# Filter products of the first batch on VectorE alone, its conversions and last inverse pair moved, second batch's units one step earlier

## Chip, cores and metric

The kernel runs on one core of a Trainium2 chip. The metric is the device time of one execution in microseconds, the median of several runs. Engines are named as in the profile: PE is TensorE (matmuls), DVE is VectorE, ACT is ScalarE, POOL is GpSimd, SP is the SyncE queue that issues most DMAs.

## The reference

Two stages in a row. The first is a global filter: a real FFT over the sequence, a product with a complex filter, and the inverse FFT. The second is an MLP with a hard-swish between two matrix products.

```python
# x (8, 3008, 256), filt_r and filt_i (1505, 256)
X = np.fft.rfft(x, axis=1)
Y = X * (filt_r + 1j * filt_i)[None]
y = np.fft.irfft(Y, n=3008, axis=1).reshape(24064, 256)
# w_in (256, 2048), w_out (2048, 256)
h = y @ w_in
g = h * np.clip(h + 3.0, 0.0, 6.0) / 6.0
out = g @ w_out
```

All inputs and the output are float32.

## The kernel before

**The transform.** 3008 is split as 47 x 64. For each of the 8 batches the first transform runs over the 47 (`a_unit`, eight chunks c for each batch; in batch 0 `a0_unit` and `turn`), its result goes to DRAM (`z_store`, tile `t1`, two buffers) and comes back in another order (`t2_load`, six chunks). Twelve `b_unit`s do the second transform, two frequencies each; `f_unit` multiplies by the filter (products of real and imaginary halves into s1 and s2), `y_unit` adds the products, `bi_unit` does the first inverse transform of a pair of units, and `g_store` writes it to DRAM. `t4_load` and `n_unit` bring it back and produce the tokens in `xn`.

**The MLP.** The tokens are handled in 47 blocks of 512 (k), each in 8 steps (p) over 256 hidden units. So there are 376 steps, counted i = 8k + p. Block 0 uses plain products (`plain_up`, `plain_down`, `plain_out`), the others a seven-product scheme (`up_1` to `up_5`, `g_sums`, `down`, `out_1` to `out_5`). In a step PE does the up product of this step and the down product of the step before. `relu` on ACT and `hswish` on DVE lie between. `store` writes a finished block to the output with up to 15 DMAs on SP; block 0's is issued in step 8.

**The weights.** Each of the 16 halves of the weights is loaded as raw bits (`w_load`) and converted by seven or eight DVE instructions (`w_ops`, L245 to L270); `w_abs` takes one of them over to ACT. POOL then forms sums of weight parts (`w_sums`, L277).

**What sets the order.** The order is written out by hand: each engine executes its instructions in the order in which the program issues them, and the DMAs of SP, ACT and POOL stand in those engines' own order. Before step 0 comes the opening: batch 0's transforms, and direct products (`direct`, `n_first`) for the first tokens. For batch 0 the filter products are split: ACT copies PSUM to SBUF (L400), POOL makes s1 (L401), DVE makes s2 (L402, L403). One conversion (w1) is issued an instruction at a time between the units of this stage, through the generator `between`; three more follow the opening. Later work is put into steps by `at(step, fn, ...)`. Functions in `EARLY` come after the up products of their step, all others at its end. For batch 1 (`places`, n == 1) the `a_unit`s lie in steps 3 to 10, the first three b units in 13, 14 and 15, and each `z_store` is issued on SP at the end of its `a_unit`'s step; `t2_load` comes a step after the last `a_unit`.

**The functions around the change.** `a0_unit` (L330), `turn` (L342), `b_unit` (L384), `f_unit`, `near` and `y_unit` (L423 to L427), `bi_unit` (L438, copies L441), `g0_first` (L448), `g_store` (L455), `t4_load` (L481), `direct` (L512), `n_first` (L519, L521), `z_store` (L373), `t2_load` (L377), `x_load` (L300), and the main program from L744 on. In steps, L537 is the up product, L563 a sum on DVE that occurs once per step from step 8 on, L587 the hard-swish, L613 the down product (L624 and L635 in block 0), L690 the output store.

Of the kernel before, what the change touches and what calls it, by code (L numbers as in the profile page):

```python
# [10 lines left out]
FP32 = mybir.dt.float32  # L11
I32 = mybir.dt.int32
AXT = mybir.ActivationFunctionType
# [10 lines left out]
NA = 47  # L24
# [90 lines left out]
def kernel(  # L115
# [117 lines left out]


    def w_conv(i):
        for _ in w_ops(i):
            pass

    def w_ops(i):
        words = st.pop(("bits", i)).rearrange("p (n two) -> p n two", two=2)  # L240
        lo, hi = words[:, :, 0], words[:, :, 1]
        big, rest = (yp.tile([P, 2, D], FP32, name="y").bitcast(I32).rearrange("p a n -> p (a n)") for j in range(2))
        v = nc.vector
        high = st.pop(("high", i), None)
        v.tensor_scalar(out=big, in0=hi, scalar1=3, scalar2=0x3FFFFFFF,  # L245
                        op0=ALU.logical_shift_left, op1=ALU.bitwise_and)
        yield
        v.scalar_tensor_tensor(out=big, in0=hi, scalar=top_c, in1=big,  # L248
                               op0=ALU.bitwise_and, op1=ALU.bitwise_or)
        yield  # L250
        v.tensor_scalar(out=rest, in0=big, scalar1=23, scalar2=23,
                        op0=ALU.logical_shift_right, op1=ALU.logical_shift_left)
        yield
        v.tensor_scalar(out=lo, in0=lo, scalar1=9, scalar2=0x3F800000,
                        op0=ALU.logical_shift_right, op1=ALU.bitwise_or)
        yield
        if high is None:
            v.tensor_scalar(out=hi, in0=hi, scalar1=1, scalar2=1,
                            op0=ALU.logical_shift_left, op1=ALU.logical_shift_right)
            high = hi.bitcast(FP32)  # L260
            yield
        rest, big = rest.bitcast(FP32), big.bitcast(FP32)
        v.scalar_tensor_tensor(out=rest, in0=lo.bitcast(FP32), scalar=1.0, in1=rest,  # L263
                               op0=ALU.subtract, op1=ALU.mult)
        yield
        v.scalar_tensor_tensor(out=rest, in0=rest, scalar=2.0 ** -20, in1=big, op0=ALU.mult, op1=ALU.add)
        yield

        two = lambda t: t.rearrange("p (a d) -> p a d", a=2)
        v.scalar_tensor_tensor(out=w_part(i)[1], in0=two(high), scalar=1.125 * 2.0 ** -15, in1=two(rest),  # L270
                               op0=ALU.is_ge, op1=ALU.mult)
        yield

    def w_sums(i, late):
        w = (w_in, w_out)[i % 2][i // 2]
# [50 lines left out]
    def a0_unit(j):  # L326
        for dh in range(2):
            ps = bank(0)
            for u in range(4):
                nc.tensor.matmul(ps[:, ts(u, P)], x0[0:64 + NA, j + u, ts(dh, P)], st["start"][0:64 + NA, ts(1, P)],  # L330
                                 start=True, stop=True)
            copy(dh and j not in (8, 12), zt(dh).rearrange("p (n j) -> p j n", j=HC)[:, j:j + 4, :],
                 ps.rearrange("p (j n) -> p j n", j=4)[:, :, 0:4 * KH])
# [54 lines left out]
    def f_unit(b, i):  # L388
        c, r = divmod(2 * i, TC)
        ps = st.pop(("ps", b, i))  # L390
        f = st["ft", b, c][:, r:r + 2, :]

        pool_, n1, n2 = (hp, "h0", "h1") if b == 0 and i & 2 else (sp, "s1", "s2")
        s1, s2 = (pool_.tile([P, 512], FP32, name=n).rearrange("p (u d) -> p u d", u=2) for n in (n1, n2))

        re, im = slice(0, HALF), slice(HALF, P)
        if b == 0:

            xf = rp.tile([P, 512], FP32, name="r", tag="r").rearrange("p (u d) -> p u d", u=2)
            nc.scalar.activation(out=xf, in_=ps, func=AXT.Copy)  # L400
            nc.gpsimd.tensor_tensor(out=s1, in0=xf, in1=f, op=ALU.mult)  # L401
            nc.vector.tensor_tensor(out=s2[re], in0=ps[re], in1=f[im], op=ALU.mult)  # L402
            nc.vector.tensor_tensor(out=s2[im], in0=ps[im], in1=f[re], op=ALU.mult)  # L403
        elif near(b, i):
            for s, part, to, x_ in (s1, re, re, re), (s1, re, im, im), (s2, im, re, im), (s2, im, im, re):
                nc.vector.tensor_tensor(out=s[to], in0=ps[x_], in1=f[part], op=ALU.mult)  # L406
        else:
            nc.vector.tensor_tensor(out=s1, in0=ps, in1=f, op=ALU.mult)
            nc.vector.tensor_tensor(out=s2[re], in0=ps[re], in1=f[im], op=ALU.mult)
            nc.vector.tensor_tensor(out=s2[im], in0=ps[im], in1=f[re], op=ALU.mult)  # L410
        st["y", b, i] = s1, s2


    def near(b, i):
        return b == 1

    def y_unit(b, i):
        s1, s2 = st["y", b, i]
        y = yp.tile([P, 2, D], FP32, name="y") if b else rp.tile([P, 512], FP32, name="r", tag="r").rearrange(
            "p (u d) -> p u d", u=2)  # L420
        re, im = slice(0, HALF), slice(HALF, P)
        if near(b, i):
            nc.gpsimd.tensor_tensor(out=y[re], in0=s1[re], in1=s2[re], op=ALU.subtract)  # L423
            nc.gpsimd.tensor_tensor(out=y[im], in0=s1[im], in1=s2[im], op=ALU.add)
        else:
            nc.vector.tensor_tensor(out=y[re], in0=s1[re], in1=s1[im], op=ALU.subtract)
            nc.vector.tensor_tensor(out=y[im], in0=s2[re], in1=s2[im], op=ALU.add)  # L427
        st["y", b, i] = y


    def bi_unit(b, i):
        ys = [st.pop(("y", b, i + v)) for v in range(2)]
        ps = [psF.tile([P, 2, D], FP32, name="psf", tag="f") for ri in range(2)]
        for v, ri in ((0, 0), (1, 0), (0, 1), (1, 1)):

            products = isinstance(ys[v], tuple)
            w, y = (wi[:, 1 + ri, :], ys[v][ri]) if products else (wi[ts(ri, 64), 0, :], ys[v][ts(ri, 64)])
            nc.tensor.matmul(ps[ri][ts(v, 64)], w, y, start=True, stop=True)  # L438
        t = t3p.tile([P, 2, 2, D], FP32, name="t3")
        for ri in range(2):  # L440
            nc.scalar.activation(out=t[:, ri, :, :], in_=ps[ri], func=AXT.Copy)  # L441
        st["t3", b, i] = t

    def g0_first(i):
        t = st["t3", 0, i]
        for v in range(2):
            for h in range(2):
                nc.scalar.dma_start(g0_d[ds(h * HC, NJ + 1), :, ds(2 * (i + v), 2), :].rearrange("c ri u d -> c ri (u d)"),  # L448
                                    t[ds(v * 64 + h * HC, NJ + 1)].rearrange("p ri u d -> p ri (u d)"))

    def g_store(b, i):
# [251 lines left out]
    with tc.manual_schedule():  # L703
# [16 lines left out]
        def load_bits(most):  # L720
            nonlocal loaded
            while loaded < most and w_before(loaded) < done:
                w_load(loaded, nc.sync)
                loaded += 1
# [38 lines left out]
        nc.sync.dma_start(wai[:, 0:8, :], wai_d[:, 0:8, :])  # L763
        load_bits(4)
        turn(0)
        between = w_ops(1)
        next(between)
        for c in range(NT):
            for i in (2 * c, 2 * c + 1):
                b_unit(0, i)  # L770
                f_unit(0, i)
                next(between, 0)
                if c == NT - 1:
                    y_unit(0, i)
            if c + 1 < NT:
                turn(c + 1)
            if c:
                bi_unit(0, 2 * c - 2)
                (g0_first if c == NT - 1 else lambda i: g_store(0, i))(2 * c - 2)
            if c == 4:  # L780
                t4_load(0, 0, KH - 3 * TC, 1)
        t4_load(0, KH - 3 * TC, KH - TC, 1)
        done = 2
        for i in 2, 3:
            w_abs(i)
        direct(NU - 2)
        direct(NU - 1)
        load_bits(8)
        nc.sync.dma_start(wa, wa_d)
        n_first()  # L790
        bi_unit(0, NU - 2)
        for i in NU - 4, NU - 2:
            g_store(0, i)
        w_abs(4)
        convert(3)
        for i in range(1, done):
            w_sums(i, False)

        def wai_load():
            nc.sync.dma_start(wai[:, 8:HC, :], wai_d[:, 8:HC, :])  # L800

        at(0, x_load, 1, 0)

        for i, s in enumerate((0, 1, 1, 2, 3, 3, 4, 4, 5, 5, 6)):
            at(s, convert_one)
# [26 lines left out]
        def places(n):  # L832
            k = first[n]
            u = [NU - 1 - i for i in range(NU)]
            b_at = [(k - 2 - j // 3) * NP + 6 - 2 * (j % 3) for j in u]

            bi_at = [b_at[i] + (5 if i % 6 == 1 else 3) for i in range(NU)]
            a_at = [(k - 7 + c // 4) * NP + (0, 2, 5, 7)[c % 4] for c in range(NB)]
            if n == 1:
                a_at = list(range(3, NB + 3))  # L840
                b_at = [13, 14, 15, 18, 19, 20, 21, 22, 26, 27, 28, 29]
                bi_at = [i + 3 for i in b_at]
            return a_at, b_at, bi_at

# [122 lines left out]
```

## Time and profile before

| what | value |
|---|---|
| median of 3 runs | 2744.99 us (2744.37 to 2745.23) |
| the profiled execution | 2745.02 us |
| its span | 2743.2 us |
| mean granted clock of PE | 0.995 |
| PE busy | 2701.6 us |
| DVE busy | 1954.4 us |
| ACT busy | 1335.9 us |
| POOL busy | 437.1 us |

The span is the stretch from the first to the last instruction of the profiled execution, and all times below are counted from its start. A busy time is the sum over an engine's instructions; an engine that is busy is not always at its peak. A line of the timeline gives start, duration, engine, source line, operation, tiles (written tile before the arrow), and in brackets how long the engine had been idle and what released it. A line of the windows gives, for one stretch, the busy time of PE, its weight load, DVE, ACT and POOL, then PE's granted clock, the DMA engines' share and the rate in GB/s.

### The profile page before, as it was taken

What the parts mean: (1) busy time and instruction counts of PE and PEld (TensorE: products, weight loads), DVE (VectorE), ACT (ScalarE), POOL (GpSimd) and SP (SyncE); (2) the same over time, 40 slices, a digit from 0 to 9 for tenths busy, and PEclk for the clock granted to TensorE, in tenths of its full rate; (3) what the DMA queues carried; (4) which work ended last, traced back from release to release, by engine and by line L of the source; (5) the groups of instructions that cost most, each with busy time, mean ns of one, the idle gap of its engine ahead of it and who ended that gap; (6) DMA issues with size and microseconds to landing.
All of it is one profiled execution on the core that took longest, in us unless ns stands there. A gap on an engine that the chain in (4) does not pass through costs nothing.

```text
span 2743.2 us, 47103 instructions
## 1 busy us (share of the span) xinstructions
PE 2701.6 (98%) x18100; PEld 2403.2 (88%) x18100; DVE 1954.4 (71%) x3384; ACT 1335.9 (49%) x2673; POOL 437.1 (16%) x634
## 2 busy tenths in 40 slices
PE   8989999999999999999999999999999999999998
PEld 5578888998899988999889998899988999999997
DVE  7958756777567875678756777577775777766665
ACT  4344455445554455444554455544545444544443
POOL 4513321101211012100121001210012100100000
PEclk9999999999999999999999999999999999999999
DMA  8633233221332113321233212332123321100000
GB/s 216 199 94 94 57 89 89 72 58 46 85 90 77 50 48 92 90 69 50 56 87 99 66 42 63 87 98 69 39 57 91 92 72 39 42 24 24 19 9 16
DMA packets 119645, 195.88 MB, mean 71 GB/s; under 512 B 21561, under 2 KB 82681, under 8 KB 119105
## 3 DMA queue, kind: packets, MB, share of 16 engines
q1 hardware_dynamic: 101627, 148.14, 19.0%
q0 software_dynamic: 17152, 44.23, 7.0%
q8 instruction: 143, 2.34, 0.4%
q14 instruction: 81, 0.66, 0.1%
q10 hardware_dynamic: 642, 0.51, 0.1%
HBM read 120.86 MB, written 71.93 MB: 70 GB/s over the span
## 4 chain that ended last, share of the span: by engine, by line
PE 93%; DVE 4%; DMA 1%; issue 1%; ACT 0%; POOL 0%; SPq 0%; POOLq 0%; DVEq 0%; ACTq 0%
PE po L613 41%; PE al L537 23%; PE be L537 17%; PE psn L491 4%; PE psf L384 2%; PE psf L361 2%; PE psf L438 2%; DVE s L406 1%; DVE g L587 1%; DMA w_all<-in_x_dram 0%; DVE y L263 0%; DMA out_dram<-o 0%; DVE g L594 0%; PE psn L512 0%; DVE y L248 0%
## 5 line engine op out<-in xcount | busy, mean ns | idle before, releaser
L613 PEld LDWEIGHTS po<-w_all,g 128*128 128x128 f32 x10304 | 1369.2, 192 | 145.5 <-issue 38.9
L613 PE MATMUL po<-w_all,g 128*128 128x128 f32 x10304 | 1400.8, 276 | 2.6 <-DVE g L587 2.4
L587 DVE SCALAR_TENSOR_TENSOR g<-r,h 128x512 f32<-128x512 f32 x736 | 511.9, 696 | 278.1 <-ACT r L582 266.5
L582 ACT ACTIVATE r<-h,half_c 128x512 f32<-128x512 f32 x736 | 531.1, 722 | 326.7 <-DVE h L563 314.7
L537 PE MATMUL al<-xt,w_all 128*128 128x256 f32 x2208 | 661.4, 381 | 9.0 <-ACT s L558 6.8
L563 DVE TENSOR_TENSOR h<-be,s 128x512 f32<-128x512 f32 x368 | 254.1, 690 | 258.6 <-PE be L537 240.4
L537 PE MATMUL be<-xn,w_all 128*128 128x256 f32 x1472 | 437.8, 379 | 0.0
L537 PEld LDWEIGHTS al<-xt,w_all 128*128 128x128 f32 x2208 | 335.7, 192 | 11.5 <-issue 9.1
L537 PEld LDWEIGHTS be<-xn,w_all 128*128 128x128 f32 x1472 | 279.7, 190 | 37.9
L577 ACT ACTIVATE h<-al 128x256 f32<-128x256 f32 x368 | 141.4, 384 | 350.8 <-PE al L537 350.8
L568 DVE TENSOR_TENSOR h<-al,s 128x256 f32<-128x256 f32 x368 | 156.2, 425 | 165.9 <-PE al L537 164.5
L595 DVE TENSOR_TENSOR g<-g 128x512 f32<-128x512 f32 x368 | 257.2, 699 | 12.6
L558 ACT ACTIVATE s<-al 128x256 f32<-128x256 f32 x368 | 141.4, 384 | 197.7 <-PE al L537 197.7
L549 ACT ACTIVATE s<-be 128x256 f32<-128x256 f32 x368 | 141.4, 384 | 176.3 <-PE be L537 176.3
L537 PE MATMUL al<-xn,w_all 128*128 128x256 f32 x736 | 219.9, 381 | 0.5 <-ACT h L577 0.5
L537 PE MATMUL be<-xt,w_all 128*128 128x256 f32 x736 | 218.9, 379 | 0.0
L373 POOL DMA_DIRECT2D z_tmp<-t x192 | 110.7, 580 | 414.6 <-ACT t L364 412.2
L548 ACT ACTIVATE s<-al 128x256 f32<-128x256 f32 x368 | 141.4, 384 | 71.0 <-PE al L537 71.0
L594 DVE TENSOR_TENSOR g<-g 128x256 f32<-128x256 f32 x368 | 162.5, 442 | 12.6
L597 DVE TENSOR_TENSOR g<-g 128x256 f32<-128x256 f32 x368 | 161.0, 438 | 12.5
L669 POOL TENSOR_TENSOR o<-p,o 128x256 f32<-128x256 f32 x45 | 32.7, 727 | 796.2 <-ACT t L441 421.7
L537 PEld LDWEIGHTS be<-xt,w_all 128*128 128x128 f32 x736 | 139.8, 190 | 18.9
(139 smaller groups left out, 1923.1 us busy)
## 6 DMA issues: line engine op xcount, KB each, us to landing
g_tmp<-t POOLq DMA_DIRECT2D x96, 256.0 KB, 3.8
t<-g_tmp SPq DMA_DIRECT2D x188, 120.0 KB
t<-z_tmp SPq DMA_DIRECT2D x42, 512.0 KB
z_tmp<-t POOLq DMA_DIRECT2D x192, 96.0 KB, 3.1
out_dram<-o SPq DMA_DIRECT2D x321, 47.0 KB
xs<-in_x_dram SPq DMA_DIRECT2D x112, 128.0 KB
ft<-in_filt_r_dram SPq DMA_DIRECT2D x88, 128.0 KB
ft<-in_filt_i_dram SPq DMA_DIRECT2D x88, 128.0 KB
```

Source lines behind the costliest of these rows:

```text
L537: nc.tensor.matmul(ps, w_in[p][:, w, :], x, start=start, stop=stop, skip_group_check=True)
L548: nc.scalar.activation(out=s[:, 0, :], in_=al, func=AXT.Copy)
L549: nc.scalar.activation(out=s5, in_=be[:, 1, :], func=AXT.Copy)
L558: nc.scalar.activation(out=s[:, 1, :], in_=al, func=AXT.Copy)
L563: nc.vector.tensor_tensor(out=st["h"][0].rearrange("p (a n) -> p a n", a=2), in0=be, in1=s, op=ALU.add)
L568: nc.vector.tensor_tensor(out=st["h"][1][:, 256:512], in0=al, in1=s5, op=ALU.add)
L582: nc.scalar.activation(out=r, in_=st["h"][i], func=AXT.Relu, bias=half_c, scale=1.0 / 6.0)
L587: nc.vector.scalar_tensor_tensor(out=st["g", k, p][:, o:o + 2, :].rearrange("p a n -> p (a n)"), in0=st["r", i], scalar=1.0, in1=st["h"][i ...
L594: v.tensor_tensor(out=g[:, G1, :], in0=g[:, G3, :], in1=g[:, G22, :], op=ALU.add)
L595: v.tensor_tensor(out=g[:, G3:G2 + 1:2, :], in0=g[:, G3:G1 + 1, :], in1=g[:, G11:G11 + 1, :].broadcast_to([P, 2, 256]), op=ALU.subtract)
L597: v.tensor_tensor(out=g[:, G4, :], in0=g[:, G12, :], in1=g[:, G2, :], op=ALU.subtract)
L613: nc.tensor.matmul(st["po", k][bank][:, part, u, :], g[:, a, ts(u, P)], w_out[p][:, w, :], start=(p == 0 and n in OPENS and u == 0), stop= ...
```

## The change

It has five parts. (1) In batch 0, `f_unit` makes all products on DVE straight from PSUM: s1 as one instruction of 128 x 512, s2 as two of 64 x 512; the ACT copy and the POOL product are gone, and no conversion instruction is issued between the units. (2) The conversion of w1 comes after the opening, with those of w2, w3 and w4 (`convert(4)`); the loads of weight bits and `x_load(1, 0)` change places on SP, and `w_abs` runs for w1 to w4. (3) The last pair's `bi_unit` and its `g_store` are put into step 0, so that on PE the pair follows the first up products. (4) Batch 1's `a_unit`s lie in steps 2 to 9, its first three b units in 12, 13 and 14, and what depends on them moves along. (5) `a0_unit`'s products have 96 columns instead of 128, and half of `g0_first`'s four DMAs are issued on SP instead of ACT.

```diff
     def w_conv(i):
-        for _ in w_ops(i):
-            pass
-
-    def w_ops(i):
         words = st.pop(("bits", i)).rearrange("p (n two) -> p n two", two=2)
...
-        yield
...
-                nc.tensor.matmul(ps[:, ts(u, P)], x0[0:64 + NA, j + u, ts(dh, P)], st["start"][0:64 + NA, ts(1, P)],
+                nc.tensor.matmul(ps[:, ds(u * P, 4 * KH)], x0[0:64 + NA, j + u, ts(dh, P)], st["start"][0:64 + NA, ds(P, 4 * KH)],
...
-        if b == 0:
-
-            xf = rp.tile([P, 512], FP32, name="r", tag="r").rearrange("p (u d) -> p u d", u=2)
-            nc.scalar.activation(out=xf, in_=ps, func=AXT.Copy)
-            nc.gpsimd.tensor_tensor(out=s1, in0=xf, in1=f, op=ALU.mult)
-            nc.vector.tensor_tensor(out=s2[re], in0=ps[re], in1=f[im], op=ALU.mult)
-            nc.vector.tensor_tensor(out=s2[im], in0=ps[im], in1=f[re], op=ALU.mult)
-        elif near(b, i):
+        if near(b):
...
-                nc.scalar.dma_start(g0_d[ds(h * HC, NJ + 1), :, ds(2 * (i + v), 2), :].rearrange("c ri u d -> c ri (u d)"),
+                (nc.scalar, nc.sync)[v].dma_start(g0_d[ds(h * HC, NJ + 1), :, ds(2 * (i + v), 2), :].rearrange("c ri u d -> c ri (u d)"),
...
-        between = w_ops(1)
-        next(between)
...
-                next(between, 0)
...
-        done = 2
-        for i in 2, 3:
+        for i in 1, 2:
             w_abs(i)
         direct(NU - 2)
         direct(NU - 1)
-        load_bits(8)
+        load_bits(6)
         nc.sync.dma_start(wa, wa_d)
         n_first()
-        bi_unit(0, NU - 2)
-        for i in NU - 4, NU - 2:
-            g_store(0, i)
-        w_abs(4)
-        convert(3)
+        g_store(0, NU - 4)
+        x_load(1, 0)
+        load_bits(8)
+        for i in 3, 4:
+            w_abs(i)
+        convert(4)
...
-        at(0, x_load, 1, 0)
+        at(0, bi_unit, 0, NU - 2)
+        at(0, g_store, 0, NU - 2)
...
-                a_at = list(range(3, NB + 3))
-                b_at = [13, 14, 15, 18, 19, 20, 21, 22, 26, 27, 28, 29]
+                a_at = list(range(2, NB + 2))
+                b_at = [12, 13, 14, 18, 19, 20, 21, 22, 26, 27, 28, 29]
```

The product that `f_unit` now uses for batch 0 stood in it before, in the last branch: `nc.vector.tensor_tensor(out=s1, in0=ps, in1=f, op=ALU.mult)` and the two lines for s2.

More of the change, by code (lines that the diff above doesn't have):

```diff
@@ L246, in w_ops @@
                         op0=ALU.logical_shift_left, op1=ALU.bitwise_and)
-        yield
         v.scalar_tensor_tensor(out=big, in0=hi, scalar=top_c, in1=big,
                                op0=ALU.bitwise_and, op1=ALU.bitwise_or)
-        yield
         v.tensor_scalar(out=rest, in0=big, scalar1=23, scalar2=23,
                         op0=ALU.logical_shift_right, op1=ALU.logical_shift_left)
-        yield
         v.tensor_scalar(out=lo, in0=lo, scalar1=9, scalar2=0x3F800000,
                         op0=ALU.logical_shift_right, op1=ALU.bitwise_or)
-        yield
         if high is None:
@@ L260, in w_ops @@
             high = hi.bitcast(FP32)
-            yield
         rest, big = rest.bitcast(FP32), big.bitcast(FP32)
@@ L264, in w_ops @@
                                op0=ALU.subtract, op1=ALU.mult)
-        yield
         v.scalar_tensor_tensor(out=rest, in0=rest, scalar=2.0 ** -20, in1=big, op0=ALU.mult, op1=ALU.add)
-        yield
         two = lambda t: t.rearrange("p (a d) -> p a d", a=2)
@@ L271, in w_ops @@
                                op0=ALU.is_ge, op1=ALU.mult)
-        yield
     def w_sums(i, late):
@@ L411, in f_unit, with near @@
         st["y", b, i] = s1, s2
-    def near(b, i):
+    def near(b):
         return b == 1
@@ L421, in y_unit @@
         re, im = slice(0, HALF), slice(HALF, P)
-        if near(b, i):
+        if near(b):
             nc.gpsimd.tensor_tensor(out=y[re], in0=s1[re], in1=s2[re], op=ALU.subtract)
```

## The prediction

> **What bounds the kernel now.** I read the page's busy shares first, then the table of windows over the first 350 us, then for each window the chain that ended last, the timeline and SP's own waits. Whole kernel: TensorE (PE) is the bound, so only PE's waits and what it does alone count.
>
> ```profile
> PE 2701.6 (98%) x18100; PEld 2403.2 (88%) x18100; DVE 1954.4 (71%) x3384; ACT 1335.9 (49%) x2673; POOL 437.1 (16%) x634
> ```
>
> By stage (us, PE busy, PEld, DVE, ACT, POOL, granted clock):
>
> ```profile
> 28.00:62.00 34.00, 28.33 (x134) 16.85 (x132) 31.55 (x36) 17.82 (x32) 20.23 (x20) 0.98 0.80 237
> 76.00:134.00 58.00, 53.44 (x200) 31.34 (x199) 53.91 (x84) 21.29 (x35) 32.93 (x53) 0.97 0.64 178
> 155.00:170.00 15.00, 8.73 (x61) 7.09 (x60) 4.21 (x8) 4.27 (x9) 0.00 (x0) 0.89 0.30 79
> 350.00:2700.00 2350.00, 2350.00 (x16074) 2127.46 (x16073) 1669.69 (x2945) 1172.55 (x2369) 305.15 (x471) 1.00 0.24 63
> ```
>
> From 350 us on PE never stops, and the change touches nothing there. What can be won lies in the opening (28 to 134 us, DVE nearly full) and in one hole at 155 to 170. The hole in the timeline, SP's queue beside it:
>
> ```profile
> 149.20 12.50 SPq L690 DMA_DIRECT2D out_dram<-o  x14
> ...
> 161.75 9.25 SPq L373 DMA_DIRECT2D z_tmp<-t  x12
> ...
> 168.34 1.08 ACT L364 ACTIVATE t<-psf 128x512 f32<-128x512 f32 x2 [7.76 <-DMA z_tmp<-t]
> ...
> 169.85 1.19 PE L537 MATMUL al<-xt,w_all 128*128 128x256 f32 x2 [6.27 <-ACT s L558]
> ```
>
> See the order: block 0's 14 output stores hold SP for 12.5 us; only then do the `z_store`s of batch 1 go out. ACT wants a `t1` buffer (two of them) for `a_unit(1,7)` in step 10; that buffer is free when `z_store(1,5)` has landed, and this store was placed in step 8, behind the output stores. ACT stands, s (L558) stands behind it, PE waits 6.27 us.
>
> The opening, DVE's own timeline:
>
> ```profile
> 38.51 3.09 DVE L258 TENSOR_SCALAR bits<-bits 128x512 int32<-128x512 int32 x1
> 41.63 0.68 DVE L402 TENSOR_TENSOR s<-po,w_all 64x512 f32<-64x512 f32 x1
> 42.34 0.69 DVE L403 TENSOR_TENSOR s<-po,w_all 64x512 f32<-64x512 f32 x1
> 43.07 3.25 DVE L263 SCALAR_TENSOR_TENSOR y<-bits,y 128x512 f32<-128x512 f32 x1
> ```
>
> Conversion instructions of 0.42 and 0.69 us last 3.09 and 3.25 while POOL's L401 products run (38.69 to 41.30, 43.17 to 45.75).
>
> **What the Trainium skill says.** "SBUF — State Buffer", Who interferes with whom: VectorE and GpSimd share one port pair as an exclusive lock; a VectorE instruction with two SBUF inputs, or in a two-port mode, contends with GpSimd, one with a single SBUF input does not. The trace agrees: L258 and L263 stretch by 2.7 and 2.6 us, L402, which reads PSUM and one SBUF operand, stays at 0.68. "TensorE: Matmul & The Clock Gate", What's actually happening: an idle array drops to half clock. The trace agrees: 0.50 between 167 and 173 us, after the hole.
>
> **Part by part.** (Steps are counted i = 8k + p.)
>
> 1. *Second batch one step back.* `a_unit(1,c)` goes from steps 3..10 to 2..9, with z stores, x loads and the first table loads. Stores 6 and 7 now stand behind the output stores; store 5, which `a_unit(1,7)` (step 9) waits for, is ahead of them. So the wait goes. One L563 runs per step: it starts at 155.43 (step 9), 169.74 (10), 178.34 (11): 22.91 us for two steps. Without hole and `a_unit`, step 10 is a plain step, 6.15 (chain: 349.86 to 356.00), and step 11 carries one n_unit, 7.27 (as 178.34 to 185.61): 13.42. **Gain 9.5 us**; in it are the 1.09 of the moved `a_unit`. That unit now lies in step 2, where PE waits for DVE (2.93 us at 94.51, after the conversions): hidden; uncovered it costs 1.09.
>    *What is late next:* `b_unit(1,0)`, moved from step 13 to 12, needs `t2_load`, which waits for all z stores. In the old times: eight z stores go out from 161.75, as `z_store` 5 and 6 did (last issue 167.2, landed 169.5 in the trace's records); `t2_load` issues at 169.6 instead of 173.1; its first 512 KB took about 3.9 us (issued 173.1; in the windows nothing moves until 175, then 363 GB/s): landed 173.5. PE reaches `b_unit` at: step 12's L563 at 155.43 + 6.15 + 7.27 + 8.2 (7.27 plus the 0.9 of a b_unit) = 177.0, less 2.4 (190.17 to 192.62 in step 13) = 174.6. Slack 1.1 us. I take no wait; bounds 0 and 3.
>    *Steps 12 to 16:* the three b units make DVE late (four L406 of 0.69 each beside POOL); 178.34 to 233.34 is 55.0 us for seven steps. The same units, n units and POOL work remain, only paired otherwise: 0, bounds -1 and +1.5. The bi_unit in step 16 instead of 17 and the earlier `t2_load`/`table_load` on SP free the queue earlier: 0.
> 2. *Filter products on DVE.* Out: 12 ACT copies L400 (0.60), 12 POOL products L401 (about 1.35, 16 us of POOL), and the eight conversion instructions between. In: 12 DVE products of 128 x 512 from PSUM. The trace has no such row; L402/L403 read the same PSUM with 512 columns at 64 partitions, 0.69, and L587 (128 x 512, one operand from PSUM) also 0.69. I take 0.69; bounds 0.65 and 0.80. Per column of two units DVE needs 6 x 0.72 = 4.3 us, PE 4.66 (31.72, 36.36, 41.02): PE sets the pace, DVE hides under it with 0.3 to spare. PE's hole at 41.02 to 48.79 (7.77) closes by 3.1. The last column starts at 31.72 + 4 x 4.66 = 50.36; its first PSUM is ready 1.05 later; DVE then runs 6 products and 4 sums, 10 x 0.72: done **58.6** (before: 62.38).
> 3. *w1's conversion joins the queue after it.* Four at 4.18 (62.38, 66.56, 70.73) = 16.7, plus about 1 for POOL's nine sums that now run beside them (one conversion beside twelve sums took 5.19 in 78.59 to 83.78): 76.3; two hswish of 0.6: 77.5, against 78.6 before: 1.1 gained. The next conversion has fewer sums beside it: +0.8. But PE finishes the first up product near 72 and then waits for DVE, so the second runs partly at half clock: -0.7. **Gain 1.2 us**, bounds -3 and +3. From there to step 7 DVE has the same eleven conversions.
> 4. *Covers.* `direct` can start at 55 instead of 59.6, `n_first` needs g0 stores and t4 loads: the two halves of `g0_first` now go on ACT and SP; SP's are behind the first `t4_load`, which leaves when POOL's stores (no longer behind L401) land. Even at 66 the first up product is at 69, far before DVE's 76: 0. `bi_unit(0,10)` (PE 1.28, two ACT copies) goes between up products of step 0 and 1, where PE waits for DVE: 0 there; ReLU must wait for it (its `r` buffer), about 73, still under 76. `g_store` waits behind 12 POOL sums, near 79; its reader `t4_load(2)` left SP at 83.2 before: 0. Bits 4 to 7, `wa` and `x_load` change order on SP within 3 us and are used 5 us or more later: 0.
> 5. *a0 with 96 columns instead of 128.* L330 at 128 columns and L491 at 94 both have median 275 ns per record: 0; at most a quarter of 7.4 us, 1.8, which the DMA of wb (landing 31.59, ahead of column 1) would swallow.
>
> Sum: 9.5 + 1.2 = 10.7. The profiled execution took 2745.02 (span 2743.2 and 1.8 around it), the median is 2744.99: the same. **2734.3 us.**
>
> **Rivals.**
> - *A: as above*, 2734.3, own range 2731 to 2738. 0.56.
> - *B: the hole moves to step 12.* Were `t2_load` to leave at 173.1 as before, it lands 177.0, 2.4 late, and the clock drop adds 1: 2737.7. For: the slack is an estimate of 1.1. Against: ACT no longer holds back the seventh store. 0.17.
> - *C: the opening gives back.* Each of the four conversions pays the 1.0 of sums that one paid, and the cold up product 1 more: the end is at 78.6 + 2.9; 9.5 - 2.9 = 6.6: 2738.4. 0.15.
> - *D: slower.* One mechanism: SP between steps 8 and 12. If each of the eight z issues waits as the longest output store did (1.95 us), they end at 177.4, land 3.6 later (chain: 164.64, 3.60), and the first t2 tile arrives with the third (6.8 after issue): 187.8. PE waits 13.2 and runs cold 2 to 4: 2750 to 2752. It decides when the tile lands after 174.6 + 10.7 = 185.3. Against: z issues took 0.3 to 0.4 unless the stores before were in flight. 0.07.
> - *E: it does not do what it says.* The hole stays because another wait was behind it (ACT frees late for another reason), and only part is gained: near 2743. Against: the releaser is named. 0.05.
>
> **How the numbers follow.** A measurement tells 0.2%, 5.5 us, from no change. Faster (below 2739.5): A 0.55, B 0.15, C 0.10 = 0.80. Within: A 0.01, B 0.02, C 0.05, D 0.02, E 0.05 = 0.15. Slower: D 0.05. Range 2729 to 2741: below, the opening's +3, step pairing and half a clock drop more; above, B and most of C; D and E stay out.
>
> **What would show it.** Right: no ACT wait on z_tmp near 160 to 170, L563 of steps 9 to 11 in 13.4 us, PE clock 1.00 there; no L400/L401, filter stage's PE columns every 4.7 us without the 7.8; first hswish about 76. Wrong: PE waiting on t2 (DMA t<-z_tmp) in step 12; filter columns paced by DVE above 4.7; hswish of step 0 after 79; a stall of PE in steps 3 to 7 on x loads or z stores.

## The result and the profile after

| what | value |
|---|---|
| median of the changed kernel, 4 runs | 2742.26 us (2734.76 to 2743.76) |
| the kernel before, beside them | 2745.11 us |
| ratio, 95% interval | 0.9984, 0.9964 to 1.0003 |
| the changed kernel in 21 further runs | 2741.02 us (2733.67 to 2745.41), ratio 0.9985, 0.9979 to 0.9992 |
| its profiled execution, and its span | 2743.62 us, 2741.8 us |
| mean granted clock of PE there | 0.993 (before 0.995) |

The forecast was 2734.3 us with a range of 2729 to 2741; both medians lie above its upper end, by 1.3 us and by 0.02 us; the two ratios, taken of the 2744.99 us that the forecast started from, give 2740.6 and 2740.9, just inside. Of the 10.7 us forecast, 2.9 and 4.1 arrived. The gain is 0.16% and 0.15%, below the 0.2% that were given as what a measurement can tell in the prediction; only the 21 further runs exclude no change. The hole is gone, as forecast. Most of what it freed was lost in the opening. Two executions marked as slow are left out of all medians and ratios: one of 3300.2 us of the kernel before with 96 columns, and one of 12414.58 us of the kernel before.

The page's busy shares of the changed kernel, and then its windows, in the stretches shown of before:

```profile
PE 2706.2 (99%) x18100; PEld 2408.9 (88%) x18100; DVE 1955.9 (71%) x3395; ACT 1329.3 (48%) x2662; POOL 423.1 (15%) x622
```

```profile
28.00:62.00 34.00, 32.05 (x150) 20.79 (x150) 26.99 (x39) 12.72 (x22) 4.75 (x8) 0.89 0.89 238
76.00:134.00 58.00, 49.96 (x184) 29.32 (x183) 51.38 (x80) 19.68 (x33) 27.19 (x43) 0.88 0.59 164
155.00:170.00 15.00, 14.38 (x83) 11.88 (x84) 7.54 (x13) 7.73 (x15) 0.46 (x1) 1.00 0.12 34
350.00:2700.00 2350.00, 2350.00 (x16075) 2127.39 (x16075) 1669.77 (x2944) 1171.85 (x2368) 306.08 (x471) 1.00 0.24 63
```

Read the third line first: between 155 and 170 PE is busy for 14.38 us instead of 8.73, at clock 1.00 instead of 0.89. The steady part is unchanged. The opening got worse: the clock is 0.89 in 28 to 62 (before 0.98) and 0.88 in 76 to 134 (before 0.97), and PE is busy for 3.5 us less in the latter. PE's busy sum is 4.6 us higher for less work: cold products last longer.

Where the hole was, the timeline of the changed kernel on SP and ACT:

```profile
151.35 2.62 SPq L361 DMA_DIRECT2D z_tmp<-t  x4
158.15 11.93 SPq L671 DMA_DIRECT2D out_dram<-o  x14
170.12 5.86 SPq L361 DMA_DIRECT2D z_tmp<-t  x8
178.26 1.49 SPq L365 DMA_DIRECT2D t<-z_tmp  x3
...
162.81 1.08 ACT L352 ACTIVATE t<-psf 128x512 f32<-128x512 f32 x2 [0.65 <-PE psf L349]
```

The output stores still hold SP for 11.9 us. But `z_store(1,5)` went out at 151.4, ahead of them; so the last `a_unit`'s ACT copy (L352, before L364) waits 0.65 us for PE, and no longer 7.76 us for z_tmp.

The sum L544 (before L563), one per step, tells gains and losses by stage:

| start of L544 in | before | after | difference |
|---|---|---|---|
| step 8 | 146.03 | 154.97 | +8.94 |
| step 11 | 178.34 | 177.78 | -0.56 |
| step 18 | 233.34 | 231.79 | -1.55 |
| span | 2743.2 | 2741.8 | -1.4 |

Steps 9 to 11 take 13.41 us instead of 22.91; in step 8 the changed kernel is already 8.94 us late. That delay is the question of the experiments. Four lines of PE's timeline show where it arises:

```profile
17.26 12.72 PE L318 MATMUL po<-p,w_all 111*128 111x96 f32 x64 [2.09 <-DMA w_all<-in_x_dram]
...
83.49 3.64 PE L605 MATMUL al<-xn,w_all 128*128 128x512 f32 x4 [5.83 <-DVE g L568]
...
107.13 2.44 PE L349 MATMUL psf<-xs,wa 47*64 47x512 f32 x8 [2.21 <-DMA xs<-in_x_dram]
109.51 6.01 PE L616 MATMUL po<-w_all,g 128*128 128x256 f32 x16
```

The last 64 of `a0_unit`'s 128 records take 12.72 us, at 96 columns; before, at 128 columns, they took 7.38:

```profile
17.98 7.38 PE L330 MATMUL po<-p,w_all 111*128 111x128 f32 x64 [0.66 <-DMA w_all<-in_x_dram]
```

Step 1's first up product runs at half clock behind a wait of 5.83 us. In step 3 PE waits 2.21 us for x, and then sixteen records of the down product take 6.01 us (3.62 when warm). By the trace's clock records the clock is halved from 18.6 us for 17.1 us, from 80.0 for 6.8 and from 107.3 for 6.8; before, it was halved three times for 3.4 us, from 13.1, 60.9 and 95.0, and from 166.7 for 6.8 in the hole and after it.

### The profile page after: what moved, and what is told of

It is laid out like the page before. It is cut to its first block, busy times and chain, and to the rows that moved or that the text cites. A ratio compares the mean times of both kernels' runs of the same rounds, so it can differ in the third digit from the quotient of the medians.

```text
span 2741.8 us, 47083 instructions
## 1 busy us (share of the span) xinstructions
PE 2706.2 (99%) x18100; PEld 2408.9 (88%) x18100; DVE 1955.9 (71%) x3395; ACT 1329.3 (48%) x2662; POOL 423.1 (15%) x622
## 4 chain that ended last, share of the span: by engine, by line
PE 94%; DVE 4%; DMA 1%; issue 1%; SPq 0%; ACT 0%; POOL 0%; POOLq 0%; DVEq 0%
PE po L594 42%; PE al L518 23%; PE be L518 17%; PE psn L472 4%; PE psf L372 3%; PE psf L349 2%; PE psf L419 2%; DVE s L387 1%; DVE g L568 0%; PE po L616 0%; PE po L318 0%; PE po L372 0%; PE al L605 0%; DMA xs<-in_x_dram 0%; DMA w_all<-in_x_dram 0%
## 5 line engine op out<-in xcount | busy, mean ns | idle before, releaser
L563 ACT ACTIVATE r<-h,half_c 128x512 f32<-128x512 f32 x736 | 531.2, 722 | 330.6 <-DVE h L544 318.6
L544 DVE TENSOR_TENSOR h<-be,s 128x512 f32<-128x512 f32 x368 | 254.1, 691 | 252.1 <-PE be L518 242.1
L576 DVE TENSOR_TENSOR g<-g 128x512 f32<-128x512 f32 x368 | 257.2, 699 | 12.6
L575 DVE TENSOR_TENSOR g<-g 128x256 f32<-128x256 f32 x368 | 162.5, 441 | 12.6
L578 DVE TENSOR_TENSOR g<-g 128x256 f32<-128x256 f32 x368 | 161.0, 437 | 12.5
```

Of the source, the lines that this page charges most:

```text
L544: nc.vector.tensor_tensor(out=st["h"][0].rearrange("p (a n) -> p a n", a=2), in0=be, in1=s, op=ALU.add)
L563: nc.scalar.activation(out=r, in_=st["h"][i], func=AXT.Relu, bias=half_c, scale=1.0 / 6.0)
L575: v.tensor_tensor(out=g[:, G1, :], in0=g[:, G3, :], in1=g[:, G22, :], op=ALU.add)
L576: v.tensor_tensor(out=g[:, G3:G2 + 1:2, :], in0=g[:, G3:G1 + 1, :], in1=g[:, G11:G11 + 1, :].broadcast_to([P, 2, 256]), op=ALU.subtract)
L578: v.tensor_tensor(out=g[:, G4, :], in0=g[:, G12, :], in1=g[:, G2, :], op=ALU.subtract)
```

## The experiments

All times are medians; a ratio is to runs of the kernel before on the same chip. The chips differ between experiments; the kernel before had medians of 2745.1 to 2745.9 us beside them, so that the ratios compare better than the medians. "Half clock" gives starts and lengths from the profiled execution.

### Did the shift do its part? Two halves of the change

*The shift alone:* the kernel before with part (4).

```diff
-                a_at = list(range(3, NB + 3))
-                b_at = [13, 14, 15, 18, 19, 20, 21, 22, 26, 27, 28, 29]
+                a_at = list(range(2, NB + 2))
+                b_at = [12, 13, 14, 18, 19, 20, 21, 22, 26, 27, 28, 29]
```

> The kernel before with part 4 alone: batch 1's a units in steps 2 to 9, its first b units in 12 to 14. Theory (the prediction's first term, 9.5, is all of the gain): no ACT wait on z_tmp in step 10, steps 9 to 11 in 13.4 us instead of 22.9, 2734 to 2736, unless x chunk 1 comes late in step 3, then 2738. Rival (the shift only pays with the queue orders of the other parts): a wait on t2 in step 12 or on x in step 3, 2738 to 2745.

Measured: 2736.58 us, ratio 0.9970 (0.9959 to 0.9982). The sum of each step (L563 here, as in the kernel before) starts at 159.78 in step 9 and at 173.19 in step 11: 13.41 us. Its window has no hole:

```profile
155.00:170.00 15.00, 14.47 (x97) 12.53 (x97) 8.21 (x15) 8.44 (x18) 0.00 (x0) 1.00 0.24 60
```

But in this profile step 8 comes 4.4 us later than before (150.39 against 146.03). In step 2 the two kernels are still level (the second up product starts at 97.50, before at 97.62); then PE waits for x in step 3, and the clock is halved from 102.4 for 6.8 us:

```profile
102.36 3.00 PE L361 MATMUL psf<-xs,wa 47*64 47x512 f32 x8 [1.89 <-DMA xs<-in_x_dram]
```

So the wait for x in step 3 comes with the shift, also where a0 has 128 columns. The profiled execution is the slowest of the six (2738.91 us).

*The opening alone:* the changed kernel with part (4) taken back, and `a0_unit` at 128 columns; so parts (1) to (3) are left, with the DMA half of (5).

```diff
-                nc.tensor.matmul(ps[:, ds(u * P, 4 * KH)], x0[0:64 + NA, j + u, ts(dh, P)], st["start"][0:64 + NA, ds(P, 4 * KH)],
+                nc.tensor.matmul(ps[:, ts(u, P)], x0[0:64 + NA, j + u, ts(dh, P)], st["start"][0:64 + NA, ts(1, P)],
...
-                a_at = list(range(2, NB + 2))
-                b_at = [12, 13, 14, 18, 19, 20, 21, 22, 26, 27, 28, 29]
+                a_at = list(range(3, NB + 3))
+                b_at = [13, 14, 15, 18, 19, 20, 21, 22, 26, 27, 28, 29]
```

> The changed kernel with a0 at 128 columns and with batch 1's units back in steps 3 to 10 and 13 to 15: parts 1 to 3 alone. Theory (DVE's work in series sets the end of the opening, and 8 us of new products plus w1's conversion weigh as much as the removed stalls): the same as before within 2 us, 2744 to 2747. Rival (the prediction's second term): faster by 1 to 3 us, 2742 to 2744.

Measured: 2745.29 us, ratio 1.0000 (0.9992 to 1.0009). The hole is back, with its releasers (ACT, then PE):

```profile
169.13 1.08 ACT L352 ACTIVATE t<-psf 128x512 f32<-128x512 f32 x2 [7.57 <-DMA z_tmp<-t]
...
170.64 1.19 PE L518 MATMUL al<-xt,w_all 128*128 128x256 f32 x2 [6.08 <-ACT s L539]
```

So the gain is the shift's, and the new opening gives nothing that can be told from none. Why the whole is not 8.2 us faster (0.30% of 2745) must then lie in the columns of a0, or in how the parts meet.

### The 96 columns

*The changed kernel with 128 columns again* (the first two lines of the diff above, nothing else):

> The changed kernel with a0's products back at 128 columns. Theory 1 (narrow products leave TensorE less busy in the a0 stage, so its clock stays halved until the turns; it cost about 5 us at 18 to 35 us): first b_unit at about 27.5 us as before instead of 32.5, clock full between 18 and 30 us, about 5 us faster than the changed kernel in its usual runs, near 2738, and runs that agree within 2 us. Rival (where the clock halves is chance, the columns have no part in it): the same spread as the changed kernel, 2735 to 2744, and a halved a0 stage in some runs.

Measured: 2735.58 us, ratio 0.9961 (0.9947 to 0.9975): 5.4 us better than the changed kernel's 2741.02 (6.6 by the two ratios). In its timeline a0 takes 9.01 us, its first part in one cold stretch of 3.4 us:

```profile
17.50 9.01 PE L318 MATMUL po<-p,w_all 111*128 111x128 f32 x64 [2.05 <-DMA w_all<-in_x_dram]
```

Its first `b_unit` starts at 28.64 and step 8's L544 at 147.42. In a second profile of the changed kernel (below), which waits for x for 0.28 us only, they start at 33.90 and 152.57: the 5.3 us of a0 arrive in step 8 almost whole.

*The kernel before with 96 columns* (the same two lines with their signs exchanged):

> The kernel before with 96 columns in a0 and nothing else changed. Theory 1: the clock is halved through the a0 stage, first b_unit at about 32.5 us instead of 27.5; slower than before by 3 to 6 us in most runs (2748 to 2751). Rival (chance): the same as before, 2745, or faster by up to 1.8 us where narrow products are quicker.

Measured: 2752.62 us, ratio 1.0025 (1.0017 to 1.0034); 6.8 us, somewhat more than the 3 to 6 expected. The clock is halved from 12.5 us for 23.9 us, though PE has work all the time:

```profile
11.24 19.75 PE L330 MATMUL po<-p,w_all 111*128 111x96 f32 x96 [1.43 <-DMA w_all<-in_x_dram]
```

A window of 18 us within this stretch, with PE busy all the time at clock 0.50:

```profile
12.60:30.60 18.00, 18.00 (x86) 17.90 (x86) 6.71 (x11) 6.43 (x8) 1.36 (x3) 0.50 0.98 220
```

*112 columns in the changed kernel* (`ds(u * P, 112)` and `ds(P, 112)`):

> The changed kernel with 112 columns in a0's products, between 96 and 128. Theory (it is the share of time in which the array streams that keeps the clock halved, and the pace is the weight load's): somewhere between; if 112 is enough, a first b_unit at 28 to 29 us and 2735 to 2736; if not, at 32 us or later and 2740 to 2744. Rival (any partial group of columns does it by its address or layout): as with 96, 2740 to 2744.

Measured: 2735.47 us, ratio 0.9966 (0.9952 to 0.9979), as good as 128. This pair is the cleanest view of the cause, since both kernels wait for the same DMA just as long before. First the changed kernel in windows of 2 us (PE's busy time, PEld, and the clock as third number from the end):

```profile
20.00:22.00 2.00, 2.00 (x11) 2.00 (x11) 0.58 (x1) 0.52 (x1) 0.00 (x0) 0.50 0.44 109
22.00:24.00 2.00, 2.00 (x11) 2.00 (x11) 0.81 (x1) 0.31 (x1) 0.00 (x0) 0.50 0.96 299
24.00:26.00 2.00, 2.00 (x12) 2.00 (x11) 0.00 (x0) 0.83 (x1) 0.00 (x0) 0.50 1.08 286
```

then 112 columns, the windows and the group of the timeline:

```profile
18.00:20.00 2.00, 2.00 (x11) 2.00 (x11) 0.00 (x0) 0.82 (x1) 0.85 (x2) 0.50 1.02 238
20.00:22.00 2.00, 2.00 (x16) 2.00 (x16) 0.83 (x1) 0.22 (x1) 0.00 (x0) 0.82 0.54 142
22.00:24.00 2.00, 2.00 (x20) 2.00 (x20) 0.83 (x1) 1.05 (x2) 0.00 (x0) 1.00 1.00 324
```

```profile
17.21 9.00 PE L318 MATMUL po<-p,w_all 111*128 111x112 f32 x64 [2.08 <-DMA w_all<-in_x_dram]
```

After a wait of 2.08 us (2.09 in the changed kernel) the clock drops in both. At 112 columns it is back 3.4 us later, at 96 columns after 17.1 us. In both, PE and its weight load are busy in every one of these windows without a gap: a "busy" PE is not enough. The pace doesn't follow the columns, 20 records in 2 us when warm at 112 columns and 21 at 128 (before, in its window 22 to 24), and the weight load is busy throughout, so I put the pace down to it. Then fewer columns only leave the products a smaller part of the same time. That this part is what the clock follows is an inference from these shapes.

*Eight solid products among the narrow ones:* the changed kernel, with one added product of 512 columns after each a0 unit. Its result is not used; this is work that the reference does not ask for.

```diff
+            if dh:
+                keep = psF.tile([P, 512], FP32, name="psf", tag="f")
+                nc.tensor.matmul(keep, st["start"][0:64 + NA, ds(P, P)], x0[0:64 + NA, j:j + 2, :].rearrange("p a d -> p (a d)"),
+                                 start=True, stop=True)
```

> The changed kernel, a0 with its 96 columns, and after each of the eight a0 units one added product of 128 x 512 on TensorE whose result nobody reads (work that the reference doesn't ask for, about 0.45 us each at full clock, 3.7 us in all). Theory: what holds the clock at half is that a0's narrow products leave the array idle too large a share of each clock window; one solid product per unit raises the share and the clock comes back in one or two windows of 3.4 us, half clock 3.4 to 7 us long, first b_unit near 28.3 + 3.7 = 32 or a little later, at most as late as the 32.5 to 34 of the narrow runs in spite of the added work. Rival: the narrow shape itself, or something outside a0, keeps the clock down: half clock for 17 to 24 us again, and with added work at half clock (0.9 each) the first b_unit at 38 or later.

Measured: 2737.14 us, ratio 0.9968 (0.9955 to 0.9980). With more work the kernel is 3.9 us faster than the changed one by the medians; all its six runs lie below 20 of the other's 21, though the intervals of the two ratios just touch. The clock does not drop in a0 at all; the first `b_unit` starts at 30.19 instead of 32.45.

```profile
23.49 1.92 PE L318 MATMUL po<-p,w_all 111*128 111x96 f32 x16
25.25 1.05 PE L322 MATMUL psf<-w_all,p 111*128 111x512 f32 x2
26.13 1.92 PE L318 MATMUL po<-p,w_all 111*128 111x96 f32 x16
```

Sixteen narrow records take 1.92 us here, 0.12 each, and 0.20 in the changed kernel: the shape itself is not slow, its clock was. An added product takes 0.88 us (25.25 to 26.13), so the eight are 7.0 us of work and not the 3.7 expected. They also filled the gap before 17 us. So this run shows that the clock is kept with them, not that they would bring it back; and it doesn't tell how much of that is the filled gap's, since the changed kernel's narrow products ran at full clock from 10 to 16 us, until the gap.

*The changed kernel once more,* to see its spread:

> The changed kernel itself, unaltered, timed five times more. If the a0 stage of 96 columns decides, its runs fall into two groups, one near 2735 to 2737 (clock back to full within a few microseconds of 18) and one near 2741 to 2744 (clock halved through a0, first b_unit after 32), median 2739 to 2743. If the spread were mere noise of the clock at large, all runs would lie within 3 us of each other.

Measured: 2741.02 us, ratio 0.9985 (0.9979 to 0.9992). The expectation of two groups failed: 19 of 21 runs lie between 2738.9 and 2744.4, one at 2733.67. In its profile the clock is halved from 13.9 for 23.9 us. Two of the longest runs (2745.41 and 2743.32) had a mean clock of 0.997, the highest of the 21, so for them a long half clock in a0 can hardly be the reason; one run of the kernel before with 96 columns was like them (2754.87 us at 0.996). No profile was taken of them, and this stays open.

### x in step 3

*`x_load(1,1)` and `(1,2)` issued with `(1,0)`, ahead of the conversions:*

```diff
-        x_load(1, 0)
+        for c in range(3):
+            x_load(1, c)
...
-        for c in 1, 2:
-            at(c, x_load, 1, c)
```

> The changed kernel with the loads of x chunks 1 and 2 of batch 1 issued with chunk 0, ahead of the weight bits that stand in SP's queue for the conversions. Theory (step 3's a_unit waits for chunk 1, 2.2 us, and the clock then halves for 7 us; about 4 us lost): no wait on DMA xs in step 3, 3 to 4 us faster than the changed kernel, near 2739 with a cold a0. Rival (the wait lies beside DVE's conversions and costs nothing): the same as the changed kernel, 2742.

Measured: 2738.90 us, ratio 0.9978 (0.9970 to 0.9985), 2.1 us below the changed kernel, with overlapping intervals. The wait is gone:

```profile
106.81 1.80 PE L349 MATMUL psf<-xs,wa 47*64 47x512 f32 x8
```

Here a0 was colder still than in the first profile (half clock for 20.5 us, first `b_unit` 1.6 us later), and yet step 8's L544 starts 2.3 us earlier, at 152.67: by this reckoning the wait and its cold tail had cost 3.9 us in that execution. In the once-more profile the same wait is 0.28 us, in that of the shift alone 1.89. So it is paid in some executions only. Its origin is SP's queue, in the first profile of the changed kernel:

```profile
96.38 0.39 SPq L226 DMA_DIRECT2D bits<-in_moe_w_in_dram  x1
97.65 0.40 SPq L226 DMA_DIRECT2D bits<-in_moe_w_out_dram  x1
98.10 8.83 SPq L288 DMA_DIRECT2D xs<-in_x_dram  x8
```

The x load stands behind loads of weight bits, which wait for conversions to free their tiles; its eight issues then need 8.83 us. With a0 at 128 columns they start at 93.10 and need 4.92; in the shift alone, also at 128 columns, 94.01 and 7.37.

*Both: 128 columns and early x loads.*

> Both of these: a0 at 128 columns and the early x loads. If both losses are real and add, 2734 to 2735 in every run, what the prediction gave and what one run of the changed kernel reached; if the clock is chance, the spread stays at 2735 to 2744.

Measured: 2734.09 us, ratio 0.9959 (0.9946 to 0.9971). Beside 128 columns alone (2735.58) the intervals overlap: what the x loads give there can't be told from nothing.

### The opening

*Kept warm:* the last kernel, with five unused products of 512 columns after `bi_unit` in step 0, again work that the reference does not ask for.

```diff
+                if p == 0:
+                    keep = psO.tile([P, 2, 2, P], FP32, name="po2").rearrange("p a u m -> p (a u m)")
+                    for j in range(5):
+                        nc.tensor.matmul(keep, w_in[0][:, 0, :], xb(0, 0), start=True, stop=True)
```

> a0 at 128 columns, early x loads, and five products of 128 x 512 into an unused PSUM bank after the moved bi_unit in step 0, while TensorE waits for DVE's conversions (their results are not used). Theory (the cold up product of step 1 costs the opening 1 to 2 us): clock full from 72 to 84 us, the hswish of step 1 about 1.2 us earlier, 2732 to 2733 instead of 2734.1. Rival (DVE is late anyway and the cold product is hidden): the same, 2734.

Measured: 2732.40 us, ratio 0.9956 (0.9943 to 0.9968), the medians 1.7 us apart, the intervals overlapping. The profiles show the effect on one place; without the added products the up products of step 1 are cold behind a wait of 5.10 us:

```profile
77.57 3.78 PE L605 MATMUL al<-xn,w_all 128*128 128x512 f32 x4 [5.10 <-DVE g L568]
81.14 2.60 PE L605 MATMUL be<-xn,w_all 128*128 128x512 f32 x4
```

with them they are not (1.88 instead of 3.78):

```profile
77.61 4.56 PE L865 MATMUL po<-xn,w_all 128*128 128x512 f32 x10
82.01 1.88 PE L605 MATMUL al<-xn,w_all 128*128 128x512 f32 x4
```

They don't show the gain of the medians. The profiled execution with the added products is the slowest of its five (2737.73 us; the others 2730.39 to 2732.76): its clock was halved from 68.4 for 6.8 us already, under step 0's up products, and step 1's hard-swish starts at 84.64, after the 82.43 without them. So the 1.7 us stand on the medians alone.

*Products on DVE, the conversion still between the units:* the kernel before with the `f_unit` of the change and nothing else.

```diff
-        if b == 0:
-
-            xf = rp.tile([P, 512], FP32, name="r", tag="r").rearrange("p (u d) -> p u d", u=2)
-            nc.scalar.activation(out=xf, in_=ps, func=AXT.Copy)
-            nc.gpsimd.tensor_tensor(out=s1, in0=xf, in1=f, op=ALU.mult)
-            nc.vector.tensor_tensor(out=s2[re], in0=ps[re], in1=f[im], op=ALU.mult)
-            nc.vector.tensor_tensor(out=s2[im], in0=ps[im], in1=f[re], op=ALU.mult)
-        elif near(b, i):
+        if near(b, i):
```

> The kernel before with batch 0's filter products on VectorE straight from PSUM, and nothing else changed: w1's conversion stays between the units, a0 keeps 128 columns, batch 1 its steps. Theory: VectorE's work in series sets the end of the opening. Each column then holds 6 products of 0.70 and about 1.3 conversion instructions that no longer stretch (0.43 to 0.70 in place of 3.09 to 3.25), so columns take about 5.0 us on VectorE, the hole of 7.8 us at the second column goes, sums end near 60 to 61 with w1 already converted, three conversions of 4.5 follow, first hswish at 75 to 77: 2742 to 2745. Rival: the opening doesn't matter at all to the end because the later conversions catch it up: 2744.5 to 2746 although the first hswish comes 2 us or more earlier.

Measured: 2743.95 us, ratio 0.9995 (0.9987 to 1.0004). The conversion instructions no longer stretch, DVE works from 30.35 to 73.00 without a pause, and the first hard-swish starts at 73.47; it was 76.20 before and 76.82 in the opening alone. Part of this lead was there at the first `b_unit`, since a0 kept its full clock in this execution: 26.26, against 27.49 before and 28.16 in the opening alone. From the fourth column on (38.71, 44.19, 49.92) the b units are 5.5 and 5.7 us apart instead of 4.66, so DVE sets their pace there. DVE in its timeline, to set beside the 3.25 us of before:

```profile
40.29 0.69 DVE L263 SCALAR_TENSOR_TENSOR y<-bits,y 128x512 f32<-128x512 f32 x1
41.02 0.69 DVE L401 TENSOR_TENSOR s<-po,w_all 128x512 f32<-128x512 f32 x1
41.74 0.68 DVE L402 TENSOR_TENSOR s<-po,w_all 64x512 f32<-64x512 f32 x1
```

Of the 2.7 us against before, 1.5 are left in step 8 (144.51 against 146.03), and about 1 in the end, too little to be told from none. The lead is still whole at step 2's first up product (91.79 against 94.51); behind the same wait as before, 2.93 us, the clock is then halved for 6.8 us instead of 3.4:

```profile
91.79 3.78 PE L617 MATMUL al<-xn,w_all 128*128 128x512 f32 x4 [2.93 <-DVE g L580]
```

*The same with the shift and the early x loads:* three edits to the kernel before. a0 at 128 columns, w1's conversion and the last inverse pair stay where they were.

> The kernel before with three edits: filter products of batch 0 on VectorE with w1's conversion still between the units, batch 1 one step back, and x_load(1,0) to (1,2) issued together ahead of the conversions. Not taken over from the change: the 96 columns, the conversion moved behind the opening, the last inverse pair in step 0. Theory: VectorE without idle time through the opening (first hswish at 73.5 as with the products alone) and the shift add up: h of step 8 near 144.5, of step 11 at 144.5 + 9.4 + 13.4 = 167.3, the constant lead over before about 9.5 + 1 + 1.5, so 2732 to 2734, no 9 us half clock in a0 and no wait for x in step 3. Rival: what the opening gains is lost again before step 8 because the eleven conversions set the pace there, 2734 to 2737, no better than the version with w1 behind the opening (2734.1).

Measured: 2731.34 us (2730.41 to 2733.38), ratio 0.9952 (0.9938 to 0.9966). It has the lowest median of all (its interval overlaps that of the kernel kept warm) and beats both kernels, 13.8 us below before. Its profiled execution is the fastest of the five. The trace shows no stretch of half clock before 2718 us. In step 2 PE now has an `a_unit` where it waited:

```profile
84.75 1.09 PE L361 MATMUL psf<-xs,wa 47*64 47x512 f32 x8
...
90.94 1.98 PE L617 MATMUL al<-xn,w_all 128*128 128x512 f32 x4 [1.44 <-DVE g L580]
```

The wait is 1.44 us instead of 2.93, the product stays warm (1.98 instead of 3.78), and step 8 comes another 3.0 us earlier (141.53). In these two profiles that is a second gain of the shift; it lasts only with x in time, for the shift alone came to step 8 4.4 us late.

## Why the prediction was right, and where it failed

The direction was right, and so was the main mechanism with its price. The size was not, since a term put at nothing took back more than half of it. That the measured times lie beside the upper end of the range is luck: it reached up to 2741 for the sake of rivals B and C, and the loss came from another place.

1. **The shift (9.5 us): right, to the tenth.** Steps 9 to 11 take 13.41 us against the 13.42 worked out, with the clock at 1.00, and `shift_alone` has 8.2 us of it in its ratio, though it pays for x in step 3. What was named as late next was not: `t2_load` left at 178.26 (the 169.6 worked out and the 8.9 us of delay make 178.5), and PE enters `b_unit` at 183.4 without a wait. So rivals B and D are out, and E too. Steps 11 to 18 take 54.0 us against 55.0, at the edge of the bounds given.
2. **Filter products (column pace 4.66, product 0.69): right.** The b units start 4.66 us apart (32.45, 37.14, 41.80, 46.47, 51.13, 55.80), and the product of 128 x 512 lasts 0.69 (L401 above). The sums end at 58.3 in the opening alone, and in the changed kernel at 64.2 instead of 58.6: 5.4 of these 5.6 us lie in the start of the last column, 55.80 instead of 50.36 (50.41 with a0 at 128 columns): point 5.
3. **w1's conversion moved (gain 1.2): mis-sized, it is 0.** `opening_alone_wide` says so (-2.5 to +2.2 us). The four conversions took 18.5 us in the changed kernel (64.20 to 82.75) instead of 17.7, and step 1's up products ran cold. The first hard-swish starts at 82.75 there, later than the 79 that the prediction named as a sign of being wrong. In `products_between`, with the conversion left between the units, it comes at 73.47, not at 76.82 as with it moved behind; of these 3.35 us 1.9 were there at the first `b_unit`. Most of the rest is in the other three conversions: they take 12.6 us there (60.36 to 73.00), before POOL's sums begin at 73.03, and 14.3 in the opening alone (62.51 to 76.83), where these sums run beside them from 66.44 on. So it is open whether the conversion's place is worth anything by itself. Rival C had this in its direction, but not as the main loss.
4. **Covers at nothing: x was not covered in the profiled execution.** "Used 5 us or more later" failed: on SP the loads of x for step 3 stood behind loads of weight bits that wait for DVE. The narrow a0 made DVE late in the changed kernel, but the shift alone has the wait too. This had been named among the signs of being wrong (a stall in steps 3 to 7 on x loads), but was given neither a price nor a chance. It cost 3.9 us with its cold tail, by the one comparison that there is.
5. **a0 at 96 columns (0, at most a gain of 1.8): this is the step that failed.** Its premise was right: the records keep one pace at 96, 112 and 128 columns when warm, so fewer columns save nothing. But a change that saves nothing was costed as one that can cost nothing, and no bound was put on the loss side. It costs 5.4 us (2741.02 against 2735.58); in the kernel before it costs 4.7 to 9.3 (the interval of 1.0017 to 1.0034). "TensorE: Matmul & The Clock Gate", What's actually happening, says that a busy window of some 3.4 us releases the throttle. In `before_narrow_a0` PE counted as busy without a gap from 12.6 to 30.6 us, five such windows in a row, and it was not released; where the page and these runs differ, the runs decide.

The sum as measured: 9.5 for the shift, nothing for the opening, less 5.4 for the 96 columns is 4.1, and 2745.1 less 4.1 is 2741.0. As the 5.4 is itself taken from 2741.02, this only says that the kernel with 128 columns has the 9.5 whole. Its profile says how: 1.4 us lost up to step 8, 9.5 gained in steps 9 to 11, 1.0 in steps 11 to 18, and a span 9.0 us shorter than before (2734.2). Without the 96 columns the changed kernel takes 2735.6, 1.3 us above the forecast; the missing 1.2 of point 3 would fill that, but the interval of its ratio is wider. No rival held the failed step: all of them were about the places that the change moves, none about a shape that it narrows.

What stays open: what exactly the clock follows between 96 and 112 columns, whether the eight products kept it by their columns or by filling the gap, and why some runs of high clock were long.

## What to carry to other kernels

A narrower product need not be free: here fewer columns saved no time and left the clock halved for a whole stage, so give such an edit a bound on the loss side. Before work is put behind a stage, look at what will run beside it there: three conversions took 12.6 us ahead of POOL's sums and 14.3 beside them. And when steps move, price every load by the queue that it stands in, with what that queue waits for, not by its distance to its use in the old times.

## What the runs showed of the hardware that was not expected

- In fp32, with a weight load for each record, products of 96 columns kept the clock at half for 17.1, 20.5, 23.9 and 23.9 us in four profiles; products of 112 (one profile) and 128 columns (five) had it back after 3.4 us, and once after 6.8; in two more profiles with 128 columns it did not drop there. All these lengths are 1, 2, 5, 6 or 7 times 3.4 us.
- Short waits were enough to lose the clock: with 128 columns it dropped in a0 after waits of 1.78 to 2.08 us (six profiles), and not after 1.69 and 1.76 (two). No limit was measured.
- Eight added products (7.0 us of work at full clock) made a kernel 3.9 us faster; five in another kernel 1.7 (there the intervals overlap).
- The conversion instruction that lasted 3.25 us beside POOL's products lasts 0.69 with POOL idle. "SBUF — State Buffer", Who interferes with whom, says so of instructions with two SBUF inputs, and the two profiles agree.
- Eight issues of the same x load on SP took 8.83 us in one kernel and 4.92 in another.
